# GpSimd makes about half of the first shifted copies of the VectorE exponentials, in an order set by the port it shares with VectorE

## The chip, the cores and the metric

The kernel runs on one core of a Trainium2 chip. Its engines are named as the profile names them: PE (TensorE, with PEld for its weight loads), ACT (ScalarE), DVE (VectorE), POOL (GpSimd) and SP (SyncE, which issues the DMAs). The metric is the device time of one launch in microseconds, lower is better; every number is the median of several runs.

## The reference

Four residual layers on a [2048, 512] bf16 activation: attention, MLP, attention, MLP with the same weights in both rounds.

```python
def _A_ref(x, wqkv, wo):
    B, S, D = x.shape
    H = 32; Dh = D // H
    qkv = (x @ wqkv).reshape(B, S, 3, H, Dh).transpose(2, 0, 3, 1, 4)
    q, k, v = qkv[0], qkv[1], qkv[2]
    scores = jnp.einsum("bhqd,bhkd->bhqk", q, k) * Dh ** -0.5
    p = _softmax(scores, axis=-1)
    o = jnp.einsum("bhqk,bhkd->bhqd", p, v)
    return o.transpose(0, 2, 1, 3).reshape(B, S, D) @ wo
def _B_ref(x, w1, b1, w2, b2):
    y = _layernorm(x, axis=-1)
    h = _gelu(jnp.einsum("bsd,df->bsf", y, w1) + b1)
    return jnp.einsum("bsf,fd->bsd", h, w2) + b2
x = x + _A_ref(_layernorm(x, axis=-1), A_wqkv, A_wo)
x = x + _B_ref(_layernorm(x, axis=-1), B_w1, B_b1, B_w2, B_b2)
x = x + _A_ref(_layernorm(x, axis=-1), A_wqkv, A_wo)
x = x + _B_ref(_layernorm(x, axis=-1), B_w1, B_b1, B_w2, B_b2)
```

With 32 heads of 16 columns and 2048 tokens, each attention layer has 32 x 2048 x 2048 exponentials. They are most of the work.

## The kernel before

The whole program is one fixed order of instructions per engine. A planner in the kernel file makes that order when the program is built: `Sched.run` holds the tasks that are pending for each engine, `Sched.best` picks the one that can start first (by priority among those that are ready), and `Prog.op` gives it a start and an end from durations that are written beside each task. Dependencies become semaphore waits in `finalize` and `emit`. On the chip only the order and the waits are left of all that.

Attention is cut into segments (`build_segments`): a segment is four heads times 512 queries (fewer at the end), and its tiles are 128 keys x 512 queries of one head. A tile goes through three steps. PE makes its scores into a PSUM bank (`score`, the matmuls under L1536). Then one of two engines makes the exponentials:

- **ACT** takes groups of three or two banks in one ACTIVATE (L1521) and writes `PT`. Such a tile costs PE one matmul with V afterwards (L1741).
- **DVE** takes a single bank (`d_load`, L1628), and adds a constant while it converts to uint16; the 16 bits are read as bf16, which gives a rough exponential. To make it exact enough, the tile is used four times, with the bits shifted by 0, 32, 64 and 96 and with V weighted to match (`vs`, made by POOL in L1287). So it costs PE four matmuls with V. Only tiles of the key blocks in `DK` (five of sixteen) may go this way; they are called D tiles here. `take_d` and `d_solo` decide when one is started: VectorE's backlog must be short, a buffer pair of `dp` and a bank must be free, at most `DFLY` = 4 pairs may be under way, and at least `DTAIL` = 8 tiles of the segment must be left.

D tiles are shifted two at a time (`DBATCH` = 2), by `job_d`. The **first shifted copy** adds 32 to the pair's 1024 columns (L1659). The **second** adds 64 to both, 2048 columns (L1667). Where two pairs are ready together the planner joins their copies into one instruction of twice the size (`mate`, `d_join`, L1614 for first and L1615 for second copies). All copies run on DVE. Copy 2 of a pair needs copy 1 and a second buffer pair.

POOL, before, scales the queries of a segment (L1262), makes the weighted V (L1287), the small chains of the norms (L941 to L946, L1095 to L1099), and merges the halves of split segments (L1784 to L1795). In the planner's model a POOL instruction with a number as `lat` lengthened the "fast" DVE instructions (the SBUF to SBUF ones) that overlap it by that number (`hits`).

`Hint.ORDER` is a string with one character for each four ACT groups. Each names one of the settings in `MODES`, which change thresholds of the planner (for how long DVE must be idle before a D tile is started, and so on).

Of the kernel before, what the change touches and what calls it, by code (L numbers as in the profile page):

```python
# [24 lines left out]
DMA_MARGIN = 1.0  # L25

# [5 lines left out]
EPS = 1e-5  # L32
RSQRT_MAGIC = float(0x5F3759DF)
# [30 lines left out]
class Prog:  # L64


    def __init__(self):
        self.streams = {e: [] for e in ENGINES}
        self.last_writer = {}
        self.readers = {}  # L70
        self.ops = []
        self.dma_rr = 0
        self.free = {e: 0.75 for e in ENGINES}
        self.bus = 0.0
        self.spare = tuple
# [30 lines left out]
    def op(self, eng, fn, reads=(), writes=(), same_ok=(), dur=0.3, lat=None):  # L106
# [12 lines left out]
        op.t0 = max(self.free[eng], self.ready(eng, reads, writes, same_ok))  # L119
        if eng == "sp":  # L120
# [158 lines left out]
class Sched:  # L279
# [237 lines left out]
DURGE = 8  # L517
PV_DEEP = 2
# [40 lines left out]
class Builder:  # L559
# [368 lines left out]
    def ln_group(self, tiles, slot, prio, eps1, eps0, shift):  # L928

        for i, tt in enumerate(tiles):  # L930
# [10 lines left out]
        yield Task("pool", prio, [I(lambda e: e.tensor_scalar(out=rs, in0=var, scalar1=eps1, scalar2=eps0, op0=ALU.mult, op1=ALU.add), [("mv", c0 + i) for i in range(n)], [R], 0.2),  # L941
                                  I(lambda e: e.tensor_tensor(out=rs, in0=rs, in1=self.cneg[:, 0:n], op=ALU.pow), [R, ("cneg",)], [R], 0.45 + 0.15 * n)])
        if shift:
            nmr = self.nmr[:, c0:c0 + n]
            yield Task("pool", prio, [I(lambda e: e.tensor_tensor(out=nmr, in0=self.mv[:, c0:c0 + n, 0], in1=rs, op=ALU.mult), [R] + [("mv", c0 + i) for i in range(n)], [("nmr", slot)], 0.2),
                                      I(lambda e: e.tensor_scalar(out=nmr, in0=nmr, scalar1=-1.0, scalar2=None, op0=ALU.mult), [("nmr", slot)], [("nmr", slot)], 0.5)])  # L946

    def ln_apply(self, tt, slot, i, dst, dres, prio, eng="dve"):
        c = 4 * slot + i
        if eng == "pool":  # L950
            return Task("pool", prio, [I(lambda e: e.tensor_scalar(out=dst, in0=self.xres[:, tt, :], scalar1=self.rs[:, c:c + 1], scalar2=self.nmr[:, c:c + 1], op0=ALU.mult, op1=ALU.add),
                                         [("x", tt), ("nmr", slot), ("rs", slot)], [dres], 0.92, (), 0.09)])
# [23 lines left out]
    def job_qkv_tile(self, L, tt, slot, i, left, prio, what):  # L976
# [80 lines left out]
        yield Task(eng, prio, [I(lambda e: e.tensor_tensor(out=sq, in0=v4, in1=v4, op=ALU.mult), [("qk", qs, k) for k in range(k0, k1)], SR, 0.14 + 0.00845 * N if eng == "dve" else 1.04)])  # L1057
# [31 lines left out]
    def bound(self, x, y, a, c, ns, dst, RQ, RN, prio, eng):  # L1089
# [4 lines left out]
        yield Task("dve", prio, [I(lambda e: e.tensor_scalar(out=yi, in0=x.bitcast(I32), scalar1=-0.5, scalar2=RSQRT_MAGIC, op0=ALU.mult, op1=ALU.add), RN, [RY], 0.21)])  # L1094
        yield Task(eng, prio, [I(lambda e: e.tensor_tensor(out=a, in0=x, in1=y, op=ALU.mult), RN + [RY], [RA], 0.34 if pool else 0.2)])  # L1095
        yield Task(eng, prio, [I(lambda e: e.tensor_tensor(out=c, in0=a, in1=y, op=ALU.mult), [RA, RY], [RC], 0.28 if pool else 0.2)])
        yield Task(eng, prio, [I(lambda e: e.tensor_scalar(out=c, in0=c, scalar1=-0.5, scalar2=1.5, op0=ALU.mult, op1=ALU.add), [RC], [RC], 0.26 if pool else 0.2)])
        yield Task(eng, prio, [I(lambda e: e.tensor_tensor(out=a, in0=a, in1=c, op=ALU.mult), [RA, RC], [RA], 0.31 if pool else 0.2)])
        yield Task(eng, prio, [I(lambda e: e.tensor_scalar(out=dst, in0=a.rearrange("p (n o) -> p n o", o=1), scalar1=-MARG, scalar2=0.0, op0=ALU.mult, op1=ALU.add),  # L1099
                                    [RA], [RQ], 0.38 if pool else 0.2)])  # L1100
# [108 lines left out]
    def job_scl(self, L, part, prio):  # L1209
# [18 lines left out]
        yield Task("pool", prio, [I(lambda e: e.tensor_tensor(out=self.kmx[:, 1:2], in0=self.kmx[:, 0:1], in1=self.chalf[0:32, :], op=ALU.pow), [("kmx", 0), ("chalf",)], [("kmx", 1)], 0.55)])  # L1228
# [24 lines left out]
    def job_qt(self, sg, s):  # L1253
# [9 lines left out]
                                  [RS, ("scl", k), ("qbias",)], [("qt", q)], 0.16 + 0.24 * W / 512 if eng == "dve" else 0.43 + 0.52 * W / 512, (), "fast" if eng == "dve" else 0.09)])  # L1263
# [8 lines left out]
    def job_vs(self, sg, i, kbs):  # L1272
# [9 lines left out]
        if L == 1:  # L1282
# [5 lines left out]
                                   [("V", hg, kb) for kb in kbs], [("vs", q, i + k2) for k2 in range(n)], 0.27 + 0.17 * n, [("vs", q, i + k2) for k2 in range(n)] if k > 1 else [], 0.09) for k in (1, 2, 3)])  # L1288
# [364 lines left out]
    def job_d(self, bt):  # L1653
# [5 lines left out]
        t = Task("dve", prio(), [I(lambda e: e.tensor_scalar(out=self.dpu(u + 1)[:, 0:N], in0=self.dpu(u)[:, 0:N], scalar1=float(SHIFT[1]), scalar2=None, op0=ALU.add),  # L1659
                                     [("dp", u, w) for w in range(n)], [("dp", u + 1, w) for w in range(n)] + self.dres(u + 1), 0.150 + 0.2605e-3 * N, (), "fast")])  # L1660
        if n == DBATCH:
            t.mate = (1, u, u)
# [12 lines left out]
        self.use_done(("dp", u))  # L1675

# [87 lines left out]
    def job_segend(self, sg):  # L1764
# [15 lines left out]
        if nparts == 2 and part == 0:  # L1780
            yield Task("dve", 1.2, [I(lambda e: e.tensor_copy(out=self.rowA[:, hg, :], in_=T[:, :, 17]), [RA], [("rowA", hg)], 0.25)])
            if L == 3:
                yield ("keys", [("oproj", 1, self.NC - 1)] + ([("retd", 0)] if DOT else []))
            yield Task("pool", 1.2, [I(lambda e: e.tensor_copy(out=M, in_=T[:, :, 0:16]), [RA], RO + [("sq", k, i) for k in (2, 3) for i in (0, 1)], 0.5), I(lambda e: e.tensor_copy(out=den, in_=T[:, :, 16]), [RA], [RD], 0.2)])  # L1784
            S_.release("accT", a)
            return
        if nparts == 2:
            dw = self.dw[:, hg % 2, :]
            RW = ("dw", hg % 2)
            yield Task("dve", 1.2, [I(lambda e: e.tensor_tensor(out=dw, in0=T[:, :, 17], in1=self.rowA[:, hg, :], op=ALU.subtract), [RA, ("rowA", hg)], [RW], 0.17)])  # L1790
            yield Task("act", -1.0, [I(lambda e: e.activation(out=dw, in_=dw, func=ACTF.Exp, scale=EXPS), [RW], [RW], 0.23)])
            yield Task("pool", 1.2, [I(lambda e: e.tensor_tensor(out=M, in0=M, in1=dw.unsqueeze(2).broadcast_to([128, 16, 16]), op=ALU.mult), [RW] + RO, RO, 0.70, (), 0.30),
                                     I(lambda e: e.tensor_tensor(out=den, in0=den, in1=dw, op=ALU.mult), [RW, RD], [RD], 0.25),
                                     I(lambda e: e.tensor_tensor(out=T[:, :, 16], in0=T[:, :, 16], in1=den, op=ALU.add), [RD, RA], [RA], 0.26),
                                     I(lambda e: e.tensor_tensor(out=T[:, :, 0:16], in0=T[:, :, 0:16], in1=M, op=ALU.add), RO + [RA], [RA], 0.75, (), 0.38)])  # L1795
        rv = self.rv[:, a, 0:nb]
        yield Task("dve", 1.2, [I(lambda e: e.reciprocal(out=rv, in_=T[:, :, 16]), [RA], [("rv", a)], 0.245)])
        if L == 3 and qc == len(self.units[3]) - 1 and hg >= 6:
            o = 2 * hg - 7
            ob = self.obl[:, :].rearrange("p (b r) -> p b r", r=32)  # L1800
            yield Task("dve", 1.2, [I(lambda e: e.tensor_tensor(out=ob[:, 0:nb, 0:16], in0=T[:, :, 0:16], in1=rv.unsqueeze(2).broadcast_to([128, nb, 16]), op=ALU.mult), [RA, ("rv", a)], [("obl",)], 0.147 + 0.268 * W / 512)])
            S_.release("accT", a)
            yield Task("dve", 1.2, [I(lambda e: e.transpose(self.OT[:, o, 0:W], self.obl[:, 0:W]), [("obl",)], [("OT", o)] + self.otd(o), 0.17 + 0.53 * W / 512)])
        else:
            if self.prev(L, qc):
                yield ("keys", [("obt",) + self.prev(L, qc)])
            yield Task("dve", 1.2, [I(lambda e: e.tensor_tensor(out=self.ob[:, 0:nb, hg, :], in0=T[:, :, 0:16], in1=rv.unsqueeze(2).broadcast_to([128, nb, 16]), op=ALU.mult), [RA, ("rv", a)], [("ob", hg)], 0.147 + 0.268 * W / 512)])
# [220 lines left out]
    def tail_tile(self, L, qc, tt, slot, i, left):  # L2028
# [18 lines left out]
        yield Task("pool", pr, [I(lambda e: e.tensor_scalar(out=rs, in0=self.mv[:, c, 1:2], scalar1=1.0 + EPS, scalar2=EPS * EPS, op0=ALU.mult, op1=ALU.add), [("mv", c)], [("rs", slot)] if i == 0 else [R], 0.25)])  # L2047
        yield Task("pool", pr, [I(lambda e: e.tensor_tensor(out=rs, in0=rs, in1=self.cneg[:, 0:1], op=ALU.pow), [("rs", slot), R, ("cneg",)], [R], 0.55)])
# [15 lines left out]
    def build(self):  # L2064
# [14 lines left out]
        self.nd = 0  # L2079
        self.build_startup()  # L2080
# [86 lines left out]
```

## Time and profile before

| | us |
|---|---|
| median of three runs | 1540.3 (1538.06 to 1541.64) |
| span of the profiled execution | 1535.9 |
| PE busy | 1486.8 |
| DVE busy | 1442.2 |
| ACT busy | 1502.5 |
| POOL busy | 343.0 |

The page gives the span of the profiled execution, and no other time of that execution; the three runs lie 2.2 to 5.7 us above this span. "Busy" counts stretches in which at least one instruction of the engine runs, so instructions that overlap their neighbours on the same engine are not counted twice. PE's busy time is not all useful: matmuls of zeros (operand `zw`, L1425 to L1429) fill its gaps.

### The profile page before, as it was taken

How to read it: one execution, taken by the hardware profiler on the slowest of the kernel's cores; microseconds unless marked ns; L12 is line 12 of the kernel's file. 1: busy time of each engine (PE TensorE's matmuls, PEld its weight loads, DVE VectorE, ACT ScalarE, POOL GpSimd, SP SyncE). 2: the span in 40 equal slices, each digit the busy share in tenths (PEclk: the TensorE clock that was granted, in tenths of full speed). 3: DMA queues.
4: the chain of work that ended last, by engine and by line, in shares of the span. 5: the costliest groups of instructions: out<-in, count | busy, mean ns of one | idle time of the engine just before them, and what ended most of it. 6: DMA issues, size and time to landing. Idle time of an engine off the chain costs nothing.

```text
span 1535.9 us, 41170 instructions
## 1 busy us (share of the span) xinstructions
PE 1486.8 (97%) x17654; PEld 491.3 (32%) x17654; DVE 1442.2 (94%) x2661; ACT 1502.5 (98%) x1346; POOL 343.0 (22%) x570
## 2 busy tenths in 40 slices
PE   9999999999999999999999999999999999999998
PEld 3222222222222222222322332222222222344555
DVE  8799999999999999999999899999999989998786
ACT  8999999999999999999999999999999999999897
POOL 3576321102120022202322138220002000020110
PEclk9999999999999999999999999999999999999999
DMA  6663102213312123214842332210011001120221
GB/s 163 120 154 91 32 22 34 51 35 68 82 48 63 37 64 84 56 35 100 138 69 64 60 87 63 53 30 18 22 36 35 14 27 32 36 49 18 73 67 30
DMA packets 212487, 90.55 MB, mean 59 GB/s; under 512 B 182251, under 2 KB 207184, under 8 KB 212304
## 3 DMA queue, kind: packets, MB, share of 16 engines
q1 hardware_dynamic: 212304, 87.92, 25.6%
q8 instruction: 138, 2.26, 0.6%
q14 instruction: 45, 0.37, 0.1%
HBM read 36.81 MB, written 19.48 MB: 37 GB/s over the span
## 4 chain that ended last, share of the span: by engine, by line
ACT 44%; PE 27%; DVE 24%; issue 3%; POOL 2%; DMA 0%; DVEq 0%; POOLq 0%
ACT PT L1521 41%; DVE dp L1628 10%; PE ps L1536 9%; PE ps L1741 8%; PE ps L1943 3%; DVE dp L1667 3%; PE ps L1882 2%; PE ps L1016 2%; ACT h L1934 2%; DVE dp L1615 2%; DVE dp L1659 1%; PE ps L1425 1%; DVE accT L1771 1%; DVE st L933 1%; DVE dp L1614 1%
## 5 line engine op out<-in xcount | busy, mean ns | idle before, releaser
L1521 ACT ACTIVATE PT<-ps 128x1536 bf16<-128x1536 f32 (+1 forms) x1256 | 1422.0, 1309 | 20.6 <-PE ps L1536 18.8
L1628 DVE TENSOR_SCALAR dp<-ps 128x512 uint16<-128x512 f32 x979 | 648.8, 679 | 33.7 <-PE ps L1536 30.4
L1536 PE MATMUL ps<-QT,KT 32*128 32x512 bf16 (+2 forms) x5120 | 602.6, 340 | 23.9 <-ACT PT L1521 7.5
L1741 PE MATMUL ps<-PT,V 128*17 128x512 bf16 (+2 forms) x3899 | 491.1, 338 | 0.6 <-issue 0.5
L1741 PE MATMUL ps<-dp,vs 128*17 128x512 bf16 (+2 forms) x3663 | 460.8, 339 | 2.7 <-issue 1.8
L1536 PEld LDWEIGHTS ps<-QT,KT 32*128 32x128 bf16 x5120 | 174.1, 91 | 543.6 <-ACT PT L1521 297.6
L1262 POOL TENSOR_SCALAR QT<-qraw,scl,qbias 128x512 bf16<-128x512 bf16 (+2 forms) x91 | 75.2, 827 | 762.8 <-PE ps L1536 754.3
L1741 PE MATMUL ps<-dp,V 128*17 128x512 bf16 (+2 forms) x1221 | 232.3, 340 | 1.6 <-DVE accT L1771 1.2
L1667 DVE TENSOR_SCALAR dp<-dp 128x2048 uint16<-128x2048 uint16 x310 | 214.3, 694 | 4.9 <-PE ps L1741 1.8
L1741 PEld LDWEIGHTS ps<-dp,vs 128*17 128x17 bf16 x3663 | 124.1, 89 | 114.1 <-issue 84.8
L1741 PEld LDWEIGHTS ps<-PT,V 128*17 128x17 bf16 x3899 | 126.9, 89 | 94.2 <-issue 75.1
L1429 PE MATMUL ps<-zw 128*32 128x448 bf16 (+23 forms) x1514 | 147.1, 322 | 0.1
L1659 DVE TENSOR_SCALAR dp<-dp 128x1024 uint16<-128x1024 uint16 (+1 forms) x298 | 126.1, 426 | 2.6
L1427 PE MATMUL ps<-zw 32*128 32x444 bf16 (+7 forms) x386 | 119.5, 332 | 0.0
L1615 DVE TENSOR_SCALAR dp<-dp 128x4096 uint16<-128x4096 uint16 x91 | 111.0, 1225 | 0.6 <-PE ps L1741 0.4
L1882 PE MATMUL ps<-yT,wf 128*128 128x512 bf16 (+5 forms) x440 | 102.7, 340 | 2.1 <-issue 1.0
L1016 PE MATMUL ps<-wqkv,xnT 128*128 128x512 bf16 x336 | 91.7, 382 | 4.1 <-DVE h L1029 1.1
L1425 PE MATMUL ps<-zw 128*128 128x448 bf16 (+14 forms) x347 | 87.4, 338 | 4.4 <-DVE onec L809 2.1
L1287 POOL TENSOR_SCALAR vs<-V 128x340 bf16<-128x340 bf16 (+2 forms) x72 | 64.3, 894 | 23.0 <-PE ps L1741 16.2
L1741 PEld LDWEIGHTS ps<-dp,V 128*17 128x17 bf16 x1221 | 58.2, 89 | 34.6 <-issue 19.4
L1614 DVE TENSOR_SCALAR dp<-dp 128x2048 uint16<-128x2048 uint16 x97 | 67.8, 700 | 0.0
L1771 DVE STREAM_TRANSPOSE accT<-ps 128x512 f32<-128x512 f32 (+2 forms) x96 | 59.2, 617 | 5.3 <-PE ps L1741 5.0
(201 smaller groups left out, 1053.4 us busy)
## 6 DMA issues: line engine op xcount, KB each, us to landing
vs<-vs_scr SPq DMA_DIRECT2D x64, 255.0 KB, 2.8
wf<-in_B_w_dram SPq DMA_DIRECT2D x90, 128.0 KB, 2.5
q_scr<-qk SPq DMA_DIRECT2D x20, 256.0 KB, 2.0
k_scr<-qk SPq DMA_DIRECT2D x12, 256.0 KB, 2.1
out_dram<-xres SPq DMA_DIRECT2D x16, 128.0 KB, 1.7
vs_scr<-vs SPq DMA_DIRECT2D x8, 255.0 KB, 3.3
xres<-in_A_x_dram SPq DMA_DIRECT2D x7, 256.0 KB, 5.3
v_scr<-vst SPq DMA_DIRECT2D x12, 136.0 KB, 1.7
```

Of the source, the lines that this page charges most:

```text
L1016: yield Task("pe", prio if c0 == 0 else min(prio, HINT.LIN2), [I(lambda e, c=c: e.matmul(self.ps[:, b, :], lhsT=xnT[:, c, :], rhs=self.wqk ...
L1425: fn = lambda e: e.matmul(self.ps[:, b, 0:w], lhsT=self.zw[:, 0:128], rhs=self.zw[:, 0:w], start=st, stop=st, skip_group_check=True)
L1427: fn = lambda e: e.matmul(self.ps[:, b, 0:w], lhsT=self.zw[32 * p:32 * p + 32, 0:128], rhs=self.zw[32 * p:32 * p + 32, 0:w], start=st, sto ...
L1429: fn = lambda e: e.matmul(self.ps[32 * p:32 * p + 32, b, 0:w], lhsT=self.zw[:, 0:32], rhs=self.zw[:, 0:w], start=st, stop=st, skip_group_c ...
L1521: S_.submit(Task("act", 1e-5 * gi, [I(lambda e, pt=pt, n=n, b0=b0: e.activation(out=self.PT[:, pt:pt + n, :], in_=self.ps[:, b0:b0 + n, :] ...
L1536: return [I(lambda e, kb=kb, i=i: e.matmul(self.ps[:, b, i * W:(i + 1) * W], lhsT=self.KT[32 * hp:32 * hp + 32, hg, kb * 128:(kb + 1) * 12 ...
L1615: return lambda e: e.tensor_scalar(out=self.both(x[1], y[1]), in0=self.both(x[0], y[0]), scalar1=float(SHIFT[2]), scalar2=None, op0=ALU.add)
L1628: self.S_.submit(Task("dve", 0.0, [I(lambda e: e.tensor_scalar(out=self.dpu(u)[:, w * 512:(w + 1) * 512], in0=self.ps[:, b, :], scalar1=BI ...
L1659: t = Task("dve", prio(), [I(lambda e: e.tensor_scalar(out=self.dpu(u + 1)[:, 0:N], in0=self.dpu(u)[:, 0:N], scalar1=float(SHIFT[1]), scal ...
L1667: t = Task("dve", prio(), [I(lambda e: e.tensor_scalar(out=self.dpp(v)[:, :, 0:N], in0=self.dpp(u)[:, :, 0:N], scalar1=float(SHIFT[2]), sc ...
L1741: ops.append((nth[j, sh] + 0.1 * i, I(lambda e, hp=hp, v=v, ap=ap[:, i * W:(i + 1) * W], first=first and i == 0, W=W: e.matmul(self.ps[32 ...
L1882: yield Task("pe", self.soft(pr if c0 == 0 else min(pr, HINT.LIN2)) if y0 == 0 else pr, [I(lambda e, c=c: e.matmul(self.ps[0:M, b, 0:W], l ...
```

## The change

The first shifted copy of a full pair is made by POOL where a new function `shifter` says so, else by DVE as before. `shifter` says POOL if at least `PURGE` = 12 tiles of the segment are left, the setting `POOL_SHIFT` is on, and POOL has nothing to do within the next 1.5 us. A copy on POOL has priority 0.6, is never joined with another, and waits not only for its data but also for the end of the last fast DVE instruction that the planner placed before it (`order`).

The planner's model of the two engines is new. Instead of `hits`, it keeps when the port that both use is taken by each. A POOL instruction's body cannot begin before the last fast DVE instruction has ended, and a fast DVE instruction's body cannot begin while POOL's body runs. `task_ready` counts this, so a fast DVE task is seen as not ready while POOL holds the port. Many small tasks are marked "fast" or "brief" and many durations are written anew. The priority of the work behind attention is 0.7 in place of 0.95 for the last queries of the first layer. `MODES` has a thirteenth setting, `c`, that turns `POOL_SHIFT` off, and `ORDER` is another string, of the same 315 characters, in which `c` stands 40 times.

```diff
+POOL_HEAD = 0.2
+DVE_HEAD = 0.137
...
             if eng == "pool":
-                self.hits = self.hits[-3:] + [(op.t0, op.t0 + dur, lat or 0.0)]
+                if lat == "after" and self.dve_port[1] is not None:
+                    order = self.dve_port[1]
+                    op.t0 = max(op.t0, order.t1 + LATENCY["pool"])
+                body = max(op.t0 + POOL_HEAD, self.dve_port[0])
+                dur = body + max(0.0, dur - POOL_HEAD) - op.t0
+                if lat != "brief":
+                    self.pool_port = (body, op.t0 + dur)
                 lat = None
             elif lat == "fast":
-                dur += sum(h for t0, t1, h in self.hits if t0 < op.t0 + dur and op.t0 < t1)
+                body = op.t0 + DVE_HEAD
+                if self.pool_port[0] <= body:
+                    body = max(body, self.pool_port[1])
+                dur = body + dur - DVE_HEAD - op.t0
+                self.dve_port = (op.t0 + dur, op)
                 lat = None
...
+        if order is not None:
+            deps[id(order)] = order
...
+            if lat == "fast":
+                r = max(r, P.pool_port[1] - DVE_HEAD)
+            elif lat == "after":
+                r = max(r, P.dve_port[0] + LATENCY["pool"])
...
+PURGE = 12
+POOL_NEAR = 1.5
...
-        t = Task("dve", prio(), [I(lambda e: e.tensor_scalar(out=self.dpu(u + 1)[:, 0:N], in0=self.dpu(u)[:, 0:N], scalar1=float(SHIFT[1]), scalar2=None, op0=ALU.add),
-                                     [("dp", u, w) for w in range(n)], [("dp", u + 1, w) for w in range(n)] + self.dres(u + 1), 0.150 + 0.2605e-3 * N, (), "fast")])
-        if n == DBATCH:
+        eng = self.shifter(sg, n)
+        t = Task(eng, prio() if eng == "dve" else 0.6, [I(lambda e: e.tensor_scalar(out=self.dpu(u + 1)[:, 0:N], in0=self.dpu(u)[:, 0:N], scalar1=float(SHIFT[1]), scalar2=None, op0=ALU.add),
+                                     [("dp", u, w) for w in range(n)], [("dp", u + 1, w) for w in range(n)] + self.dres(u + 1), 0.150 + 0.2605e-3 * N if eng == "dve" else 0.34 + 0.834e-3 * N, (), "fast" if eng == "dve" else "after")])
+        if n == DBATCH and eng == "dve":
             t.mate = (1, u, u)
...
+    def shifter(self, sg, n):
+
+        S_ = self.S_
+        if n < DBATCH or not HINT.POOL_SHIFT or self.left(sg) < PURGE:
+            return "dve"
+        near = S_.now + POOL_NEAR
+        if self.P.free["pool"] > near or any(S_.task_ready(t) <= near for t in S_.pend["pool"]):
+            return "dve"
+        self.npool += 1
+        return "pool"
...
-        return 0.95 if L == 1 and qc >= self.NC - 2 or L == 3 and qc >= LATE3 else 2.2
+        return 0.7 if L == 1 and qc == self.NC - 1 else 0.95 if L == 1 and qc >= self.NC - 2 or L == 3 and qc >= LATE3 else 2.2
```

More of the change, by code (lines that the diff above doesn't have):

```diff
@@ L119, in op @@
         op.t0 = max(self.free[eng], self.ready(eng, reads, writes, same_ok))
+        order = None
         if eng == "sp":
@@ L1056, in job_qkv_tile @@
         eng = "pool" if what == "kv" else "dve"
-        yield Task(eng, prio, [I(lambda e: e.tensor_tensor(out=sq, in0=v4, in1=v4, op=ALU.mult), [("qk", qs, k) for k in range(k0, k1)], SR, 0.14 + 0.00845 * N if eng == "dve" else 1.04)])
+        yield Task(eng, prio, [I(lambda e: e.tensor_tensor(out=sq, in0=v4, in1=v4, op=ALU.mult), [("qk", qs, k) for k in range(k0, k1)], SR, 0.14 + 0.00845 * N if eng == "dve" else 1.04, (), "fast" if eng == "dve" else None)])
         if "k" in what:
@@ L1093, in bound @@
         pool = eng == "pool"
[L1094 to L1098, printed above, removed]
+        yield Task("dve", prio, [I(lambda e: e.tensor_scalar(out=yi, in0=x.bitcast(I32), scalar1=-0.5, scalar2=RSQRT_MAGIC, op0=ALU.mult, op1=ALU.add), RN, [RY], 0.17, (), "fast")])
+        yield Task(eng, prio, [I(lambda e: e.tensor_tensor(out=a, in0=x, in1=y, op=ALU.mult), RN + [RY], [RA], 0.25 if pool else 0.2, (), "brief" if pool else "fast")])
+        yield Task(eng, prio, [I(lambda e: e.tensor_tensor(out=c, in0=a, in1=y, op=ALU.mult), [RA, RY], [RC], 0.25 if pool else 0.2, (), "brief" if pool else "fast")])
+        yield Task(eng, prio, [I(lambda e: e.tensor_scalar(out=c, in0=c, scalar1=-0.5, scalar2=1.5, op0=ALU.mult, op1=ALU.add), [RC], [RC], 0.22 if pool else 0.2, (), "brief" if pool else "fast")])
+        yield Task(eng, prio, [I(lambda e: e.tensor_tensor(out=a, in0=a, in1=c, op=ALU.mult), [RA, RC], [RA], 0.25 if pool else 0.2, (), "brief" if pool else "fast")])
         yield Task(eng, prio, [I(lambda e: e.tensor_scalar(out=dst, in0=a.rearrange("p (n o) -> p n o", o=1), scalar1=-MARG, scalar2=0.0, op0=ALU.mult, op1=ALU.add),
[L1100 removed]
+                                    [RA], [RQ], 0.33 if pool else 0.2, (), "brief" if pool else "fast")])
     def job_first_tile(self, tt, slot, i, left, prio):
@@ L1262, in job_qt @@
         yield Task(eng, 0.4, [I(lambda e: e.tensor_scalar(out=self.QT[:, q, 0:W], in0=src, scalar1=self.scl[:, k, hg:hg + 1], scalar2=self.qbias[:, 0:1], op0=ALU.mult, op1=ALU.add),
-                                  [RS, ("scl", k), ("qbias",)], [("qt", q)], 0.16 + 0.24 * W / 512 if eng == "dve" else 0.43 + 0.52 * W / 512, (), "fast" if eng == "dve" else 0.09)])
+                                  [RS, ("scl", k), ("qbias",)], [("qt", q)], 0.16 + 0.24 * W / 512 if eng == "dve" else 0.34 + 0.43 * W / 512, (), "fast" if eng == "dve" else None)])
         if s is None:
@@ L1287, in job_vs @@
         yield Task("pool", 0.8, [I(lambda e, k=k: e.tensor_scalar(out=self.vs[:, q, k - 1, i:i + n, :], in0=src, scalar1=WSHIFT[k], scalar2=None, op0=ALU.mult),
-                                   [("V", hg, kb) for kb in kbs], [("vs", q, i + k2) for k2 in range(n)], 0.27 + 0.17 * n, [("vs", q, i + k2) for k2 in range(n)] if k > 1 else [], 0.09) for k in (1, 2, 3)])
+                                   [("V", hg, kb) for kb in kbs], [("vs", q, i + k2) for k2 in range(n)], 0.21 + 0.17 * n, [("vs", q, i + k2) for k2 in range(n)] if k > 1 else []) for k in (1, 2, 3)])
         for kb in kbs:
@@ L2046, in tail_tile @@
         rs = self.rs[:, c:c + 1]
-        yield Task("pool", pr, [I(lambda e: e.tensor_scalar(out=rs, in0=self.mv[:, c, 1:2], scalar1=1.0 + EPS, scalar2=EPS * EPS, op0=ALU.mult, op1=ALU.add), [("mv", c)], [("rs", slot)] if i == 0 else [R], 0.25)])
-        yield Task("pool", pr, [I(lambda e: e.tensor_tensor(out=rs, in0=rs, in1=self.cneg[:, 0:1], op=ALU.pow), [("rs", slot), R, ("cneg",)], [R], 0.55)])
+        yield Task("pool", pr, [I(lambda e: e.tensor_scalar(out=rs, in0=self.mv[:, c, 1:2], scalar1=1.0 + EPS, scalar2=EPS * EPS, op0=ALU.mult, op1=ALU.add), [("mv", c)], [("rs", slot)] if i == 0 else [R], 0.25, (), "brief")])
+        yield Task("pool", pr, [I(lambda e: e.tensor_tensor(out=rs, in0=rs, in1=self.cneg[:, 0:1], op=ALU.pow), [("rs", slot), R, ("cneg",)], [R], 0.55, (), "brief")])
         xr = yield ("get", "xn")
```

40 lines of the change are left out of this document (21 added, 19 removed).

## The prediction

> **What bounds the kernel now.** I read the page's busy shares first, then its costliest groups, then the busy time in windows of 50 us.
>
> ```profile
> PE 1486.8 (97%) x17654; PEld 491.3 (32%) x17654; DVE 1442.2 (94%) x2661; ACT 1502.5 (98%) x1346; POOL 343.0 (22%) x570
> ...
> ACT 44%; PE 27%; DVE 24%; issue 3%; POOL 2%; DMA 0%; DVEq 0%; POOLq 0%
> ...
> L1521 ACT ACTIVATE PT<-ps 128x1536 bf16<-128x1536 f32 (+1 forms) x1256 | 1422.0, 1309 | 20.6 <-PE ps L1536 18.8
> L1628 DVE TENSOR_SCALAR dp<-ps 128x512 uint16<-128x512 f32 x979 | 648.8, 679 | 33.7 <-PE ps L1536 30.4
> ```
>
> ACT is full: 1422.0 us of its 1502.5 are exponentials, and it waits 20.6 us for scores. Its own chain is the largest part of the chain that ended last. The line with 979 loads says how many tiles DVE takes off ACT. What follows is that time is gained when ACT gets fewer tiles, and ACT gets fewer when DVE can take more. By shapes, ACT's groups are:
>
> ```profile
> L1521 ACT ACTIVATE PT<-ps 128x1536 bf16<-128x1536 f32 x605 | 924.6, 1528 | 14.6 <-PE ps L1536 13.2
> L1521 ACT ACTIVATE PT<-ps 128x1024 bf16<-128x1024 f32 x651 | 712.5, 1105 | 5.9 <-PE ps L1536 5.7
> ```
>
> 605 x 3 + 651 x 2 = 3117 tiles, so a tile costs ACT 1422.0 / 3117 = 0.456 us. In the windows (columns: length, then busy time of PE, PEld, DVE, ACT, POOL):
>
> ```profile
> 100.00:150.00 50.00, 46.94 (x459) 13.69 (x461) 49.61 (x106) 49.12 (x47) 33.48 (x76) 1.00 0.48 121
> ...
> 300.00:350.00 50.00, 49.02 (x500) 14.39 (x497) 46.61 (x82) 49.91 (x43) 2.65 (x2) 1.00 0.11 30
> ...
> 1100.00:1150.00 50.00, 48.64 (x579) 14.71 (x578) 49.89 (x84) 50.00 (x46) 1.89 (x2) 1.00 0.14 30
> ...
> 1250.00:1300.00 50.00, 49.89 (x453) 14.02 (x445) 45.22 (x82) 49.25 (x46) 1.32 (x2) 1.00 0.10 27
> ...
> 1350.00:1400.00 50.00, 48.74 (x932) 22.72 (x935) 48.52 (x90) 49.78 (x45) 8.54 (x12) 1.00 0.17 37
> ```
>
> Of the 26 windows from 100 to 1400 us, DVE is busy at least 49.0 us in thirteen. There DVE and ACT are at their limits together. In the other thirteen (46.61 at 300, 45.22 at 1250) ACT is as full as ever while DVE has time left: there something else holds D tiles back, such as buffers, banks or PE. DVE time freed in these windows buys little. POOL, outside the stages that make norms and keys, is nearly idle (1.32 to 8.54 us of 50).
>
> **The copies moved.** The groups by shape, and three of the lines by themselves (minimum/median/maximum ns):
>
> ```profile
> L1667 DVE TENSOR_SCALAR dp<-dp 128x2048 uint16<-128x2048 uint16 x305 | 212.2, 699 | 4.9 <-PE ps L1741 1.8
> L1659 DVE TENSOR_SCALAR dp<-dp 128x1024 uint16<-128x1024 uint16 x293 | 124.7, 429 | 2.6
> L1615 DVE TENSOR_SCALAR dp<-dp 128x4096 uint16<-128x4096 uint16 x91 | 111.0, 1225 | 0.6 <-PE ps L1741 0.4
> L1614 DVE TENSOR_SCALAR dp<-dp 128x2048 uint16<-128x2048 uint16 x97 | 67.8, 700 | 0.0
> ...
> L1659 DVE TENSOR_SCALAR dp<-dp x298: 250/417/840, 86.4 to 1517.2; 128x1024 uint16<-128x1024 uint16 x144, 128x512 uint16<-128x512 uint16 x5
> L1667 DVE TENSOR_SCALAR dp<-dp x310: 380/683/1157, 87.6 to 1517.7; 128x2048 uint16<-128x2048 uint16 x151, 128x1024 uint16<-128x1024 uint16 x4
> L1614 DVE TENSOR_SCALAR dp<-dp x97: 622/682/1133, 153.7 to 1459.5; 128x2048 uint16<-128x2048 uint16 x97
> ```
>
> Instructions of one engine overlap, so I take what each holds DVE from start to start, in a stretch of its timeline:
>
> ```profile
> 586.56 0.41 DVE L1659 TENSOR_SCALAR dp<-dp 128x1024 uint16<-128x1024 uint16 x1
> 586.89 0.68 DVE L1628 TENSOR_SCALAR dp<-ps 128x512 uint16<-128x512 f32 x1
> 587.49 0.68 DVE L1667 TENSOR_SCALAR dp<-dp 128x2048 uint16<-128x2048 uint16 x1
> 588.09 0.71 DVE L1771 STREAM_TRANSPOSE accT<-ps 128x512 f32<-128x512 f32 x1
> ```
>
> A single first copy holds DVE 0.33 us, a load 0.60, a second copy 0.60. A joined first copy has the second copy's size and duration, so 0.60; a joined second one is 1.225 long, less the same overlap of 0.08: 1.14.
>
> There are 293 + 2 x 97 = 487 full pairs. Their first copies hold DVE 293 x 0.33 + 97 x 0.60 = 154.9 us. Half of them, 243, go to POOL. Of the 244 left, fewer find a partner: if the share that is joined halves from 40% to 20%, 24 joined and 196 single ones hold 24 x 0.60 + 196 x 0.33 = 79.1. **Freed: 76 us of DVE.** Second copies are left as they are.
>
> **What the copy costs POOL.** No copy of this shape runs there. The nearest row is the query scaling, one SBUF input, two bytes in and out:
>
> ```profile
> L1262 POOL TENSOR_SCALAR QT<-qraw,scl,qbias x91: 447/767/2122, 40.6 to 1502.9; 128x512 bf16<-128x512 bf16 x67, 128x128 bf16<-128x128 bf16 x16, 128x256 bf16<-128x256 bf16 x8
> ...
> L1057 POOL TENSOR_TENSOR h<-dp 128x512 bf16<-128x512 bf16 x2 | 2.2, 1086 | 1.3 <-DVE dp L1022 1.3
> ```
>
> The minimum is that of 128 columns, the median that of 512: (767 - 447) / 384 = 0.83 ns a column, so 1024 columns take 0.767 + 512 x 0.00083 = 1.19 us. The two-input row, 1.09 us for 512, is the far end: about 2.1 us if uint16 ran at its speed. I take 1.19, as the operation is the scaling's. 243 x 1.19 = 289 us fit into POOL's idle 1193 us.
>
> **What the port costs.** The timeline shows both engines holding each other up:
>
> ```profile
> 939.17 0.62 POOL L1792 TENSOR_TENSOR dp<-dp,dw 128x256 f32<-128x256 f32 x1 [1.11 <-ACT dw L1791]
> 939.42 0.92 DVE L1614 TENSOR_SCALAR dp<-dp 128x2048 uint16<-128x2048 uint16 x1
> ...
> 941.49 1.18 DVE L1615 TENSOR_SCALAR dp<-dp 128x4096 uint16<-128x4096 uint16 x1
> 941.52 1.80 POOL L1262 TENSOR_SCALAR QT<-qraw,scl,qbias 128x512 bf16<-128x512 bf16 x1
> ```
>
> The DVE copy that began inside a POOL instruction took 0.92 in place of 0.68; POOL's scaling that began behind a DVE copy took 1.80 in place of 0.77, and ended 0.65 us after that copy. So the two do not run side by side, they run one after the other. The Trainium skill says the same ("SBUF — State Buffer", section "Who interferes with whom": the pair of ports is held for the whole instruction, and the other engine blocks). It goes on against this change ("Perfetto Trace Analysis", section "Optimizing Scalar/DVE Operations"): moving work between the two "might not help". That result is the second rival below.
>
> How often does a copy hit? All of before's excess over the medians is (429 - 417) x 293 + (699 - 683) x 305 + (700 - 682) x 97 + (1225 - 1215) x 91 = 11 us. The last term's median is in the row below, as is POOL's busy time from 150 us on:
>
> ```profile
> L1615 DVE TENSOR_SCALAR dp<-dp x91: 1162/1215/1590, 154.9 to 1460.9; 128x4096 uint16<-128x4096 uint16 x91
> ...
> sum 1386.00, PE 1345.88 PEld 445.66 DVE 1310.45 ACT 1361.90 POOL 254.56; mean PE 224.31 PEld 74.28 DVE 218.41 ACT 226.98 POOL 42.43
> ```
>
> 11 us over 255 us of POOL is 0.043 us a microsecond; 289 us more of it cost 12 us of DVE. The new order, which starts POOL right behind a fast copy and lets DVE load meanwhile, could bring this to nothing: two loads, 1.20 us, fill such a copy's time. The far end is random placement. After the move DVE starts some 24 + 196 + 305 + 91 = 616 fast copies in about 1430 us, one in 2.3. Of POOL's 1.19 us about 1.0 holds the port, so 0.43 fast copies fall into it and wait 0.5 us on average: 0.21 x 243 = 52 us. I take 12, as the order is chosen with the port in view: **64 us net.**
>
> **From DVE time to ACT time.** A further D tile holds DVE for a load, half of a second copy and what is left of first copies: 0.60 + (305 x 0.60 + 91 x 1.14) / 979 + 79 / 979 = 0.97 us, and takes 0.456 off ACT. Both ends stay level if n x (0.97 + 0.456) = 64, n = 45 tiles, 20 us. With nothing lost to the port it is 76 / 1.43 = 53 tiles, **24 us**, the most this can give. As DVE is at its limit in half the windows, I take half: **10 us**. PE pays three more matmuls with V per tile; it has matmuls of zeros to give up for them.
>
> **The edits without a price.** The POOL copy waits for a DVE instruction, and behind it on POOL stand the scaling of the next segment's queries and the small chains. POOL waited 754.3 us for PE before the scalings, as they are made long ahead:
>
> ```profile
> POOL QT L1262 <- PE ps L1536: 754.3, 58, 32.3
> ```
>
> Two microseconds more are covered by that; if the cover is gone, scores wait for them and ACT idles, up to 2 us in each of the 91 segments. A pair's first copy lands about 1.2 us later than on DVE, and the second copy with it, under the limit of four pairs under way. A pair is due each 1440 / 490 = 2.9 us, so four allow 12 us each; I cost it at nothing, and what is late next is a free `dp` buffer. The new string and durations only reorder work. At best they remove ACT's idle 1535.9 - 1502.5 = 33 us, at worst they add as much; I take zero, for nothing in the trace prefers an end. The priority 0.7 acts around 850 to 1000 us, where ACT idles 5.0 us (145.03 busy of 150): zero to 5 us, taken as zero.
>
> ```profile
> 850.00:1000.00 150.00, 145.04 (x1482) 43.63 (x1474) 136.69 (x252) 145.03 (x136) 62.55 (x105) 1.00 0.30 66
> ```
>
> DMAs, SP's queue and the second copies' engine stay as they are. The sum: 1535.9 - 10 = 1526 for the profiled span; the median of the runs is 4.4 us above that span, so **1540.3 - 10 = 1530 us**.
>
> **The rivals.**
>
> - *All of it converts:* the windows with DVE time left have it only because of the old order. 20 to 24 us, 1516 to 1520. For it: ACT is full in both kinds of window, so each further D tile pays at once. Against: 45.22 of 50 at 1250 us, with ACT at 49.25.
> - *No change:* either the random price, 52 us, is paid and the remaining 24 of DVE are worth 24 / 1.43 x 0.456 = 8 us in full and 4 by half, less small waits; or D tiles are limited by buffers and PE everywhere. 1537 to 1543, say 1540. The same comes out if POOL's turn is rarely free and few copies move.
> - *Slower, by the port as a queue:* a POOL copy takes the port just when the second copy of another pair comes up. DVE works in order, so the loads behind it wait too, their PSUM banks stay taken, and ACT gets the tiles. The break-even is 76 / 243 = 0.31 us of stall per moved copy. At 0.45 us the loss is 109 - 76 = 33 us of DVE, 33 / 1.43 x 0.456 = 10.5 us: 1551. A POOL copy at 2.1 us would do this: the port is held almost twice as long, and two loads no longer fill it. For it: L1659's maximum of 840 ns and the scaling's of 2122. Against: the average hit so far is small.
>
> **How the numbers follow.** Forecast, 1520 to 1537: 0.50. All converts: 0.12. No change: 0.20. Slower: 0.18. This kernel's measurement can tell about 0.2%, 3 us, from no change. So faster 0.62, same 0.20, slower 0.18. The range goes from the full 24 us, 1516, to 1546, past the no-change cases and half way into the slower one.
>
> **What would show it.** L1659 on POOL about 240 times at 1.2 us; on DVE L1659 and L1614 together near 220; L1628 about 1000 to 1025 times and ACT's tiles fewer by as many; L1667's mean below 740 ns. If L1667's mean rises to 800 or more, the port takes the gain. If L1628 stays at 979 while DVE's idle time grows, D tiles were limited elsewhere. If POOL's copies last 2 us, the size from the scaling was wrong.

## The result and the profile after

| | before | after |
|---|---|---|
| median, us | 1539.33 (4 runs) | 1818.89 (4 runs, 1811.92 to 1828.84) |
| ratio | | 1.182 (1.178 to 1.186) |
| span of the profiled execution | 1535.9 | 1827.1 |

The change makes the kernel 280 us slower, far outside the range I gave. The page of the kernel after, its busy times, chain and costliest groups:

```profile
PE 1591.6 (87%) x17479; PEld 502.3 (27%) x17607; DVE 1423.7 (78%) x2534; ACT 1528.5 (84%) x1346; POOL 1074.0 (59%) x825
...
POOL 34%; DVE 31%; PE 27%; issue 5%; ACT 3%; DMA 0%; DVEq 0%; POOLq 0%
...
L1543 ACT ACTIVATE PT<-ps 128x1536 bf16<-128x1536 f32 (+1 forms) x1256 | 1447.7, 1236 | 284.6 <-PE ps L1558 280.2
L1682 POOL TENSOR_SCALAR dp<-dp 128x1024 uint16<-128x1024 uint16 x255 | 713.8, 2805 | 553.0 <-DVE dp L1650 360.3
L1650 DVE TENSOR_SCALAR dp<-ps 128x512 uint16<-128x512 f32 x997 | 662.6, 682 | 132.5 <-PE ps L1558 124.3
```

ACT's groups wait 284.6 us where they waited 20.6, nearly all of it for scores. These 264 us are most of the 291 by which the two spans differ; another 26 us are ACT's busy time, which grew from 1502.5 to 1528.5 with the same number of instructions. POOL, which did not appear in the chain with more than 2%, now leads it with 34%. 255 copies were moved, where 243 were forecast, but each takes 2805 ns in place of the 1.19 us that I worked out and the 1.194 that the planner writes beside the task. The line by itself (minimum/median/maximum ns):

```profile
L1682 POOL TENSOR_SCALAR dp<-dp x255: 2762/2770/3736, 121.2 to 1802.0; 128x1024 uint16<-128x1024 uint16 x128
```

And who waits for whom (us in total, times, longest):

```profile
POOL dp L1682 <- DVE dp L1650: 360.3, 105, 16.5
ACT PT L1543 <- PE ps L1558: 280.2, 307, 8.9
...
DVE dp L1690 <- POOL dp L1682: 166.2, 129, 3.0
...
PEld ps L1775 <- POOL dp L1682: 121.5, 98, 3.3
...
PE ps L1775 <- POOL dp L1682: 79.3, 74, 3.1
```

The copies' minimum is 2762: this is no stall of a few copies, each copy is that long. Behind it wait DVE's second copies (L1690), 166.2 us, and PE's work with V (L1775): 121.5 us before its weight loads and 79.3 before its matmuls, two waits that can overlap. Both engines work in order, so the loads on DVE and the scores on PE that stand behind wait as well, and ACT waits for those scores. The granted clock of PE fell too, from 0.999 before, and a score matmul takes 354 ns on average where it took 340. How much of the loss goes through this slower clock was not separated from the waits themselves:

```profile
core 0: 1827.1 us, clock 0.940
```

### The profile page after: what moved, and what is told of

Same layout as the page of the kernel before. It is cut to its first block, busy times and chain, and to the rows that moved or that the text cites. A ratio compares the mean times of both kernels' runs of the same rounds, so it can differ in the third digit from the quotient of the medians.

```text
span 1827.1 us, 41062 instructions
## 1 busy us (share of the span) xinstructions
PE 1591.6 (87%) x17479; PEld 502.3 (27%) x17607; DVE 1423.7 (78%) x2534; ACT 1528.5 (84%) x1346; POOL 1074.0 (59%) x825
## 4 chain that ended last, share of the span: by engine, by line
POOL 34%; DVE 31%; PE 27%; issue 5%; ACT 3%; DMA 0%; DVEq 0%; POOLq 0%
POOL dp L1682 29%; DVE dp L1650 12%; PE ps L1775 9%; PE ps L1558 9%; DVE dp L1690 6%; ACT PT L1543 2%; DVE dp L1637 2%; PE ps L1977 2%; PE ps L1038 2%; PE ps L1916 2%; DVE dp L1682 1%; POOL QT L1284 1%; PE ps L1447 1%; DVE h L1945 1%; DVE accT L1805 1%
## 5 line engine op out<-in xcount | busy, mean ns | idle before, releaser
L1543 ACT ACTIVATE PT<-ps 128x1536 bf16<-128x1536 f32 (+1 forms) x1256 | 1447.7, 1236 | 284.6 <-PE ps L1558 280.2
L1682 POOL TENSOR_SCALAR dp<-dp 128x1024 uint16<-128x1024 uint16 x255 | 713.8, 2805 | 553.0 <-DVE dp L1650 360.3
L1558 PE MATMUL ps<-QT,KT 32*128 32x512 bf16 (+2 forms) x5120 | 640.3, 354 | 71.9 <-DVE dp L1650 56.4
L1775 PE MATMUL ps<-dp,vs 128*17 128x512 bf16 (+2 forms) x3735 | 524.5, 358 | 86.7 <-POOL dp L1682 79.3
L1775 PE MATMUL ps<-PT,V 128*17 128x512 bf16 (+2 forms) x3875 | 514.7, 350 | 0.4 <-issue 0.4
L1690 DVE TENSOR_SCALAR dp<-dp 128x2048 uint16<-128x2048 uint16 (+1 forms) x370 | 264.0, 719 | 173.2 <-POOL dp L1682 166.2
L1775 PE MATMUL ps<-dp,V 128*17 128x512 bf16 (+2 forms) x1245 | 251.5, 359 | 3.8 <-DVE accT L1805 2.1
L1775 PEld LDWEIGHTS ps<-dp,vs 128*17 128x17 bf16 x3735 | 132.7, 90 | 256.0 <-POOL dp L1682 121.5
L1451 PE MATMUL ps<-zw 128*32 128x448 bf16 (+18 forms) x1404 | 168.3, 345 | 6.0 <-DVE dp L1650 6.0
L1775 PEld LDWEIGHTS ps<-PT,V 128*17 128x17 bf16 x3875 | 125.2, 89 | 95.3 <-issue 79.5
L1449 PE MATMUL ps<-zw 32*128 32x444 bf16 (+2 forms) x408 | 135.0, 355 | 0.0
L1447 PE MATMUL ps<-zw 128*128 128x448 bf16 (+15 forms) x316 | 84.8, 358 | 11.6 <-DVE dp L1650 7.7
L1682 DVE TENSOR_SCALAR dp<-dp 128x1024 uint16<-128x1024 uint16 (+1 forms) x175 | 77.3, 444 | 1.1
L1775 PEld LDWEIGHTS ps<-dp,V 128*17 128x17 bf16 x1245 | 58.6, 89 | 45.9 <-issue 24.8
L1945 DVE TENSOR_SCALAR h<-ps,b1c 128x512 bf16<-128x512 f32 (+4 forms) x88 | 57.6, 655 | 11.1 <-PE ps L1916 10.6
```

What stands on the lines that cost most here:

```text
L1449: fn = lambda e: e.matmul(self.ps[:, b, 0:w], lhsT=self.zw[32 * p:32 * p + 32, 0:128], rhs=self.zw[32 * p:32 * p + 32, 0:w], start=st, sto ...
L1451: fn = lambda e: e.matmul(self.ps[32 * p:32 * p + 32, b, 0:w], lhsT=self.zw[:, 0:32], rhs=self.zw[:, 0:w], start=st, stop=st, skip_group_c ...
L1543: S_.submit(Task("act", 1e-5 * gi, [I(lambda e, pt=pt, n=n, b0=b0: e.activation(out=self.PT[:, pt:pt + n, :], in_=self.ps[:, b0:b0 + n, :] ...
L1558: return [I(lambda e, kb=kb, i=i: e.matmul(self.ps[:, b, i * W:(i + 1) * W], lhsT=self.KT[32 * hp:32 * hp + 32, hg, kb * 128:(kb + 1) * 12 ...
L1682: t = Task(eng, prio() if eng == "dve" else 0.6, [I(lambda e: e.tensor_scalar(out=self.dpu(u + 1)[:, 0:N], in0=self.dpu(u)[:, 0:N], scalar ...
L1775: ops.append((nth[j, sh] + 0.1 * i, I(lambda e, hp=hp, v=v, ap=ap[:, i * W:(i + 1) * W], first=first and i == 0, W=W: e.matmul(self.ps[32 ...
```

## The experiments

Two theories. **A:** the loss is the copy's duration against its plan; the fixed order has no room for 1.58 us more per copy. **B:** copies on POOL cost this by themselves, by the port or by the time that a pair is under way. A third possibility is that the other edits (string, model, priority) carry part of it.

### e0: what the forms of the copy cost

Eight forms on POOL, behind the last output of the kernel before. `T16`, `TB` and `T32` are the same bytes read as uint16, bf16 and int32; `sc` and `sc2` hold one float per partition.

```diff
+        forms = [
+            lambda e: e.tensor_scalar(out=T16(1), in0=T16(0), scalar1=32.0, scalar2=None, op0=ALU.add),
+            lambda e: e.tensor_scalar(out=T16(1), in0=T16(0), scalar1=32.0, scalar2=0.0, op0=ALU.add, op1=ALU.add),
+            lambda e: e.tensor_scalar(out=T16(1), in0=T16(0), scalar1=sc, scalar2=None, op0=ALU.add),
+            lambda e: e.tensor_scalar(out=T16(1), in0=T16(0), scalar1=sc2, scalar2=sc, op0=ALU.mult, op1=ALU.add),
+            lambda e: e.tensor_scalar(out=TB(1), in0=TB(0), scalar1=32.0, scalar2=None, op0=ALU.add),
+            lambda e: e.tensor_scalar(out=TB(1), in0=TB(0), scalar1=0.5, scalar2=1.0, op0=ALU.mult, op1=ALU.add),
+            lambda e: e.tensor_scalar(out=TB(1), in0=TB(0), scalar1=sc2, scalar2=sc, op0=ALU.mult, op1=ALU.add),
+            lambda e: e.tensor_tensor(out=T32(1), in0=T32(0), in1=self.c32[:, 0:1].broadcast_to([128, 512]), op=ALU.add),
+        ]
```

> The kernel before, with eight forms of the copy on POOL, three instructions each, behind the last output, so that nothing runs beside them; its own work is unchanged. What sets the 2.77 us of the copy of 1024 uint16 columns? (a) The type: then all four uint16 forms take about 2.77 and the bf16 forms about 1.19. (b) The one operation with an immediate, as in the weighting of V, which also costs about 2.5 ns a column on bf16: then one operation with an immediate takes 2.77 on both types, and two operations or per-partition scalars about 1.19. (c) Three passes over any 1024 columns: all seven take 2.77. The eighth form, an int32 add of 512 columns with a constant column, has half as many columns and two inputs: about 1.1 us by the two-input bf16 row of before.

The groups of POOL by shape in the tail of e0. The lines stand in the order of cost; L2119 is the first form of the list, L2126 the last:

```profile
L2120 POOL TENSOR_SCALAR dp<-dp 128x1024 uint16<-128x1024 uint16 x3 | 10.9, 3633 | 0.2
L2121 POOL TENSOR_SCALAR dp<-dp,row 128x1024 uint16<-128x1024 uint16 x3 | 8.5, 2842 | 0.3
L2119 POOL TENSOR_SCALAR dp<-dp 128x1024 uint16<-128x1024 uint16 x3 | 8.4, 2784 | 0.3
L2123 POOL TENSOR_SCALAR dp<-dp 128x1024 bf16<-128x1024 bf16 x3 | 8.3, 2769 | 0.3
L2125 POOL TENSOR_SCALAR dp<-dp,onesm,row 128x1024 bf16<-128x1024 bf16 x3 | 3.6, 1200 | 0.3
L2122 POOL TENSOR_SCALAR dp<-dp,onesm,row 128x1024 uint16<-128x1024 uint16 x3 | 3.6, 1195 | 0.3
L2124 POOL TENSOR_SCALAR dp<-dp 128x1024 bf16<-128x1024 bf16 x3 | 3.1, 1047 | 0.2
L2126 POOL TENSOR_TENSOR dp<-dp,c 128x512 int32<-128x512 int32 x3 | 3.1, 1039 | 0.2
```

(The whole of e0 took 1590.35 us, with this tail.) None of my three answers is right as a whole; of (b) the half on one operation with an immediate held. Type does not decide (2784 on uint16, 2769 on bf16), nor does immediate against per-partition scalar (2784 against 2842), nor the number of operations: two additions take 3633. What is fast is the pair multiply, then add: 1047 with immediates, 1195 to 1200 with per-partition scalars, on both types where it was tried. The query scaling, from which I took 1.19, is that pair. The copy is one addition. A multiplication alone was not among the forms, but the weighting of V (L1287) is one, and the trace of before has it slow as well, as the account of the prediction shows below.

### e1 and e2: the rest of the edits, and a planner that knows the duration

e1 turns `POOL_SHIFT` off in all settings. e2 changes one planned duration:

```diff
-    0.150 + 0.2605e-3 * N if eng == "dve" else 0.34 + 0.834e-3 * N
+    0.150 + 0.2605e-3 * N if eng == "dve" else 0.21 + 2.5e-3 * N
```

> The changed kernel with POOL_SHIFT off in all settings: no copy goes to POOL; the new port model, durations, priority and string stay. If the copies on POOL carry the loss: 1525 to 1560. If the string, the model or the priority carry a large part of it: above 1650.

> The changed kernel with one number of the planner mended: a first copy on POOL is planned at 0.21 + 2.5 ns a column, 2.77 us for 1024, in place of 1.19. Theory A, the order is laid out for copies of 1.19 us and each copy comes 1.58 us late for everything behind it: 1520 to 1570, with ACT waiting for scores below 60 us. Theory B, a copy of 2.77 us is too slow whatever the order, by the port it holds and the time a pair is under way: above 1650 and ACT still waiting more than 150 us for scores.

| | us | ratio to before |
|---|---|---|
| e1, no copy on POOL | 1593.83 | 1.037 (1.035 to 1.039) |
| e2, copies planned at 2.77 | 1608.26 | 1.046 (1.044 to 1.049) |

Both lie between what I expected of the theories. I had left out that any edit to the plan shifts the whole order, so that the string, made for one exact plan, no longer fits. For e1 the runs show it: the same kernel without any string (e6 below) takes 1583.99 us, 10 less. For e2 it is likely but was not tested. Against each other they do say something. In e2, 204 copies of 2.80 us run on POOL, ACT waits only 47.5 us for scores, and it is 14 us slower than with no copy on POOL at all. So slow copies that the planner knows of cost little; theory B as I put it, above 1650, falls.

```profile
L1682 POOL TENSOR_SCALAR dp<-dp 128x1024 uint16<-128x1024 uint16 x204 | 571.7, 2804 | 470.5 <-DVE dp L1650 302.8
...
ACT PT L1543 <- PE ps L1558: 47.5, 82, 13.6
```

### e3: the same order with the fast form

Order, planned times and string of the kernel after; only the form of the copy on POOL is another, and its result the same bits.

```diff
+        how = one if eng == "dve" else dict(scalar1=1.0, scalar2=float(SHIFT[1]), op0=ALU.mult, op1=ALU.add)
```

> The changed kernel, same order of all instructions, string and planned times; only the form of the copy on POOL differs: multiply by 1 and then add 32, in place of one add. The result is the same bits. e0 showed 1.05 to 1.20 us for a multiply and add of 1024 columns, near the 1.19 that the plan counts with. Theory A, the loss is the copy's duration against its plan: 1505 to 1540, ACT waiting for scores below 50 us, and the prediction's steps can be read here as they were meant. Theory B, moving copies to POOL costs by port and waits even at the planned duration: above 1560.

Measured: **1544.64 us** (12 runs), ratio 1.0036 (1.0023 to 1.0049) to 1538.88 of before. The page of e3:

```profile
PE 1483.9 (96%) x17607; PEld 486.4 (32%) x17607; DVE 1392.1 (91%) x2534; ACT 1496.9 (97%) x1346; POOL 600.7 (39%) x825
...
L1543 ACT ACTIVATE PT<-ps 128x1536 bf16<-128x1536 f32 (+1 forms) x1256 | 1416.5, 1280 | 27.5 <-PE ps L1558 23.9
L1650 DVE TENSOR_SCALAR dp<-ps 128x512 uint16<-128x512 f32 x997 | 660.7, 681 | 77.8 <-PE ps L1558 70.5
...
L1684 POOL TENSOR_SCALAR dp<-dp 128x1024 uint16<-128x1024 uint16 x255 | 268.0, 1051 | 699.7 <-DVE dp L1650 438.5
```

The same 255 copies in the same order at 1.05 us take away 274 of the 280 us. ACT's wait for scores falls from 280.2 to 23.9. So the loss comes with the copy's duration, in this order; and as e2's copies of that duration cost little once the plan counted with them, the two runs together show theory A. The third possibility falls with it, as the string, the model and the priority stay in e3, and e3 is 6 us from before. It also shows what the change would bring as it was meant: nothing, and slightly the wrong way. DVE has 50 us less to do (1442.2 to 1392.1) and loads 18 more tiles (979 to 997), ACT's exponentials take 5.5 us less (1422.0 to 1416.5). But ACT's idle time grows from 1535.9 - 1502.5 = 33.4 to 1538.0 - 1496.9 = 41.1 us, by 7.7. As ACT is busy 5.6 us less in all, 2.1 us are left, the difference of the two spans. The profiled execution took 1540.11 us, so the trace shows 2.1 of the 5.8 us by which the medians differ. One place is the stretch from 900 to 950 us, in before (first) and in e3:

```profile
900.00:950.00 50.00, 48.22 (x529) 14.96 (x530) 45.51 (x85) 47.33 (x45) 34.82 (x59) 1.00 0.36 91
```

```profile
900.00:950.00 50.00, 47.32 (x504) 15.46 (x497) 43.09 (x84) 44.97 (x43) 32.70 (x63) 1.00 0.40 90
```

ACT (fourth engine column) loses 2.4 us there, though DVE is less busy too. What holds it up in this stretch I did not test.

### e4 to e6: without strings

e4 is the kernel before with `ORDER = ''`, e5 is e3 with it, e6 the kernel after with no copy on POOL and with it.

> The kernel before with an empty string: every step has the first setting. I priced a new string at nothing. If that holds also for having none: 1535 to 1550. e1 and e2 (1594 and 1608 us, whose string was made for another plan) suggest that the string is worth tens of microseconds: 1570 to 1610.

> As e3_form, copies on POOL by multiply and add, with an empty string. Beside e6_off_nostring it gives what the copies on POOL are worth on an equal footing. If they bring what I worked out for DVE (10 us, at most 24): 10 to 24 us below e6_off_nostring. If the port takes the gain back: equal or above.

> The changed kernel with no copy on POOL and an empty string: what is left is the new port model, the durations and the priority. If these are neutral: within 10 us of e4_before_nostring, and near e1_pool_off (1594).

| | us | ratio to before |
|---|---|---|
| e4, before, no string | 1600.20 | 1.040 (1.038 to 1.041) |
| e6, after, no copy on POOL, no string | 1583.99 | 1.029 (1.027 to 1.030) |
| e5, after, fast copies on POOL, no string | 1579.32 | 1.025 (1.024 to 1.027) |

The string of before is worth 61 us (1600.20 - 1538.88); that of after, with fast copies, 35 us (1579.32 - 1544.64). The new model, durations and priority together gave 16 us (e4 to e6, where I had expected at most 10), the copies on POOL 4.7 us (e6 to e5, where I had expected 10 to 24). The groups of DVE's loads and the busy times, e6 first:

```profile
PE 1532.2 (97%) x17905; PEld 507.3 (32%) x17905; DVE 1428.6 (90%) x2636; ACT 1524.2 (96%) x1350; POOL 334.8 (21%) x570
...
L1650 DVE TENSOR_SCALAR dp<-ps 128x512 uint16<-128x512 f32 x952 | 632.9, 680 | 64.2 <-PE ps L1558 60.2
```

```profile
PE 1532.7 (97%) x17919; PEld 506.5 (32%) x17919; DVE 1353.6 (86%) x2428; ACT 1518.5 (96%) x1345; POOL 677.6 (43%) x905
...
L1650 DVE TENSOR_SCALAR dp<-ps 128x512 uint16<-128x512 f32 x968 | 645.1, 682 | 118.7 <-PE ps L1558 107.0
```

DVE is busy 75 us less although it loads 16 tiles more; by the prediction's 1.43 us a tile, 75 / 1.43 = 52 further tiles would have kept both ends level. DVE's loads now wait 107.0 us for scores, before 60.2: the time is there, the scores are not. Each single comparison of two orders carries the accident of the order, so neither 16 nor 4.7 us is safe as what the edits are worth in another order.

### e7: the copy longer still

The order of after once more, with two additions, 3.63 us.

```diff
+        how = one if eng == "dve" else dict(scalar1=float(SHIFT[1]), scalar2=0.0, op0=ALU.add, op1=ALU.add)
```

> The changed kernel, same order, with the copy on POOL as two additions (32, then 0), which e0 showed at 3.63 us against 2.78 for one. From e3_form (1.05 us, 1545) to the change (2.77 us, 1819) 255 copies became 1.72 us longer and the kernel 274 us: 0.62 us of each late microsecond. Theory A, each late microsecond of a copy is paid because the order has no room for it: 255 x 0.86 x 0.62 = 136 us more, 1955, and more if the room that some copies had is used up (to 2030). Theory B, the loss comes from the port or from the number of copies and not from their length: 1819 to 1850.

Measured: 2053.32 us (2 runs), ratio 1.335 (1.330 to 1.340). The line by itself:

```profile
L1684 POOL TENSOR_SCALAR dp<-dp x255: 3622/3628/4677, 121.3 to 2022.9; 128x1024 uint16<-128x1024 uint16 x128
```

ACT's wait for scores, and then the granted clock:

```profile
ACT PT L1543 <- PE ps L1558: 492.8, 389, 11.2
```

```profile
core 0: 2049.8 us, clock 0.884
```

0.86 us more on 255 copies is 219 us of POOL, and the kernel lost 234: 1.07 us for each late microsecond, where the step from 1.05 to 2.77 cost 274 / (255 x 1.72) = 0.62. The result is above my upper bound of 2030. That the room that some copies had is used up, so that the whole delay is now the kernel's, would fit a share of 1. It does not explain more than 1, and the granted clock fell further, from 0.940 to 0.884, with score matmuls of 370 ns where after had 354. How much each adds was not separated. Theory B's 1850 is far off.

## Why the prediction was wrong

**What the copy costs POOL** is the step that failed. I wrote: "I take 1.19, as the operation is the scaling's." It was not: the scaling multiplies and adds, the copy only adds, and e0 shows 1.05 to 1.20 us for the one and 2.78 for the other. My far end, 2.1 us from a two-input row, was too low as well. The sign that I had named for this, copies that last 2 us, came with 2.77. The trace of before held the right neighbour, the weighting of V, one operation with one constant:

```profile
L1287 POOL TENSOR_SCALAR vs<-V 128x340 bf16<-128x340 bf16 x24 | 28.6, 1192 | 7.2 <-PE ps L1741 6.1
...
L1287 POOL TENSOR_SCALAR vs<-V 128x136 bf16<-128x136 bf16 x24 | 15.7, 658 | 1.1
```

(1192 - 658) / 204 = 2.6 ns a column, three times the scaling's 0.83; 1024 columns would have been 2.97 us. I picked the neighbour by size and type when the operation differed, and never asked which of two rows on the same engine was alike in that.

**The slower rival,** given 0.18, named the sign and the trigger ("A POOL copy at 2.1 us would do this") and priced it at 10.5 us. It counted only DVE's stalls and let ACT take the tiles over, at 0.32 us of time per DVE microsecond. On the chip nobody takes anything over: the order is fixed, PE stands before a matmul whose operand is late, and the scores behind it wait. The runs show 0.62 to 1.07 us per late microsecond of a copy.

**The count, 243,** came out as 255, **DVE's first copies** as 160 single and 38 joined ones or 160 x 0.33 + 38 x 0.60 = 75.6 us, forecast 79.1. These steps were right.

**The price of the port,** 12 us, cannot be read in after, whose order is disturbed, but it can in e3. The same sum of means over medians there is (702 - 684) x 355 + (436 - 418) x 160 + (739 - 683) x 38 + (1262 - 1217) x 68 = 14 us, 3 more than before, and DVE's second copies wait another 3.0 us for POOL: about half of the 12. The net of 64 us holds as well, as DVE is busy 50 us less and has 18 tiles more, which at 0.97 us are 17.5: 68 us. **From DVE time to ACT time:** I forecast 22 more tiles and 10 us. e3 has 18 more tiles, and 5.5 us less of exponentials, but 7.7 us more idle time on ACT, so nothing is left. My halving was near for the tiles; the idle time is the term that was missing. With copies even a little shorter than I had taken them, e3 took 1544.64 us, to which the *no change* rival, 1537 to 1543, comes nearest; so the gain of 10 us would have failed here too. What keeps DVE's free time from becoming tiles stays open: neither more buffers nor another limit was tried.

**The string at nothing,** with bounds of 33 us, was mis-sized. On the path through the runs without strings, exchanging the one (61 us) for the other (35 us) loses 27, and the new model and the copies gain 16 + 5, which leaves the 6 us by which e3 is behind. A string's worth also hangs on every planned duration, as e1 and e2 show, so it cannot be priced as a part by itself. It is not what made the kernel 280 us slower: e3 with the same string lies 6 us from before.

## What to carry to other kernels

Price an operation on a new engine by a row of that engine with the same operation, not only the same size and type; where two rows of one engine differ threefold per column, find out which of them is yours. In a program whose order is laid out ahead, a wrong duration in the plan is paid even on an engine that has time to spare, since every engine waits in order: here 0.62 to 1.07 us of the kernel for each late microsecond on an engine that was never more than 63% busy. 204 slow copies that were planned for cost 14 us against none on POOL, 255 that were not cost 274 against fast ones. And settings that were searched on an exact plan belong to that plan; to judge an edit, compare without them.

## What the runs showed of the hardware

**POOL has a fast form of `tensor_scalar`.** Multiply then add runs at about 1.05 us for 1024 columns with constants, one addition at 2.77, two additions at 3.63 (e0, e3, e7). The Trainium skill ("GPSIMD Engine Reference", section 4.1) calls one-input work on this engine roughly line-rate; the trace agrees for multiply and add (0.83 ns a column in the query scaling) and not for one operation (2.6 ns in the weighting of V). An int32 add of a tensor and one constant column moves the same bytes in 1.04 us.

**The slow form does not hold the port throughout.** The Trainium skill ("SBUF — State Buffer", section "Who interferes with whom") has the port held for the whole instruction. In the timeline of after, three second copies meet a POOL copy:

```profile
335.40 2.77 POOL L1682 TENSOR_SCALAR dp<-dp 128x1024 uint16<-128x1024 uint16 x1
335.47 1.51 DVE L1690 TENSOR_SCALAR dp<-dp 128x2048 uint16<-128x2048 uint16 x1 [0.25 <-POOL dp L1682]
...
707.01 2.77 POOL L1682 TENSOR_SCALAR dp<-dp 128x1024 uint16<-128x1024 uint16 x1 [6.79 <-DVE dp L1682]
708.04 0.68 DVE L1690 TENSOR_SCALAR dp<-dp 128x2048 uint16<-128x2048 uint16 x1
...
1306.11 2.77 POOL L1682 TENSOR_SCALAR dp<-dp 128x1024 uint16<-128x1024 uint16 x1 [5.63 <-DVE dp L1637]
1307.99 1.43 DVE L1690 TENSOR_SCALAR dp<-dp 128x2048 uint16<-128x2048 uint16 x1
```

The one that starts 0.07 us into the copy takes 1.51 in place of 0.68, so it gets the port about 0.9 us in, 1.9 us before POOL is done. The one that starts 1.03 us in is not held up at all. The one that starts 1.88 us in takes 1.43 and ends 0.54 us after POOL. So the port is taken at the beginning and at the end and is free between. The rest of the timeline bears the three lines out. Of the 52 shifted copies of DVE that it shows starting inside one of POOL's, the 10 in its first 0.64 us are held up, by 0.26 to 0.84 us; the 28 that start 0.82 to 1.63 us in are late by at most 0.07; and of the 14 from 1.88 us on, 13 end 0.28 to 0.58 us after POOL (the last one met a POOL copy stretched to 3.64 us and was not held). In e7, with copies of 3.63 us, the free stretch is longer: DVE's copies that start 0.91 to 2.63 us in are late by at most 0.04, and those of 2.78 to 3.31 us wait until POOL is done. A DVE copy in the free stretch can delay POOL in turn: one that starts 1.62 us in and takes its usual 0.68 goes with a POOL copy of 3.19. That POOL reads, computes and writes in turn would fit all this and the threefold time; it was read from timelines and not tested by an edit.
